# Value sums of three late periods in two halves of the rows, with dense half products between them

## The chip, the core and the metric

The kernel runs on one core of a Trainium2 chip. The metric is the device time of one execution in microseconds, the median of three runs. One more execution was taken with the hardware profiler; its trace is what the times of single instructions come from.

## What is computed

The reference mixes two branches of the same input x (2048 tokens, 512 features) by a gate per token. Branch a is softmax attention with 32 heads of 16 features, branch b a gated layer of width 1792:

```
q, k, v = split(x @ wqkv)                         # 32 heads of 16
p = softmax(q @ k^T / 4);  a = (p @ v) @ wo
b = (sigmoid(x @ w_gate) * (x @ w_up)) @ w_down
g = sigmoid(sum(x * gate_w));  out = g * a + (1 - g) * b
```

All of it is float32. Dense products are made of split operands (a high and a low part, three products for one), in the fast float32 form of TensorE; the value sums p @ v are in plain float32, which TensorE runs in two passes for each product.

## The kernel before

**Periods.** The attention runs in 256 periods (`NPER`), k from 0 to 255, sixteen for each of 16 pairs of heads. Period k takes two key tiles of 128 keys, 1024 queries and the two heads of its pair. Its scores are eight products of 64 rows on 512 queries (line 679, `st_part`): four for the first head of the pair on TensorE's rows 0 to 63 (`t0`, period k) and four for the second on rows 64 to 127 (`t1`, made one period ahead, for k + 1). ScalarE takes the exponential of each into a tile `p` (line 681). `values(k)` (line 823) then sums over the keys: for each of the two key tiles (a = 0, 1) four products of 128 rows, one for each head and half of the queries (c = 3 to 0), with 16 value columns and a column of ones, so 17 columns, which go to partitions 32c of one bank (line 831). The sum leaves its bank by `put` (line 836 on ScalarE, from period 245 on line 838 on VectorE) and is added to a running sum on GpSimd, one period later (line 848).

**Dense half products.** Beside the scores, which use half of TensorE's rows, dense products of the other branches run in halves of the rows. `Sum.half(g)` (line 159) gives one product of 64 rows, on the lower rows (`d0`, g = 0) or the upper (`d1`, g = 1); a `Sum` has six of each, which add up in the one bank `dn`. Where a `Sum` goes from the upper rows to the lower, or back, `turn` (line 171) puts an empty instruction on GpSimd that waits for the last product of the one half, and the first of the other half waits for it: both halves write one bank and must not do so at once. When a `Sum` is done, the next one is fetched from a generator (line 911), and in fetching it the finished one is copied out of `dn` (line 469; from period 245 on that copy, `leave`, is on VectorE). In the last periods the Sums are those of the heads' output projection (`hp`, weights `wo0`, `wo1`).

**Order.** Every engine but the DMA queues runs in the order in which the program issues. The order within a period is written by hand as a string of words, which `emit` (line 870) reads: `t0` and `t1` a score product with its exponential, `d0` and `d1` a half product, `m0` and `m1` a product for the maxima of a later period with its reduction on VectorE, `turn` the change of rows, together with GpSimd's waiting work of about 2 us. `STEADY` serves the periods before 245 (`FREE`) and holds six `d1` and six `d0`, one `Sum` for each period. `LAST` serves the eleven periods from 245 on, in which no maxima are left:

```
LAST = "t0 d1 t0 d1 t0 d1 turn t0 t1 t1 d0 t1 d0 t1 d0"
```

With three `d1` and three `d0` a `Sum` takes two periods: 245 and 246, 247 and 248, and so on to 253 and 254. Behind the words of a period come, in this order: the fetch of the next `Sum` if one is done, or a `turn` if one is half done; GpSimd's waiting work (line 916); `values(k)` (line 925); and from period 245 on three steps of `early` (line 939), VectorE's work on the first hidden tiles (lines 761 to 774: reciprocals, products, splits). In these periods score products and value sums take their banks in turn from the seven banks other than `dn` (`bank7`, line 709).

**After the periods** come the down products (line 1021) with the value sum of period 255 between them, which fill TensorE to the end of the kernel, and the rest of the output projection.

Of the kernel before, what the change touches and what calls it, by code (L numbers as in the profile page):

```python
# [21 lines left out]
SHARED = "both halves of the PE write one bank"  # L22
SYNC = mybir.DependencyInfo(mybir.DependencyClass.Sync, mybir.DependencyReason.DATA)

S, D, H, DH, F = 2048, 512, 32, 16, 1792
P = 128
# [5 lines left out]
VW = DH + 1  # L32
# [6 lines left out]
FREE = NPER - LEAD // 2  # L39
# [7 lines left out]
def gated_mix(ctx, tc, x, xT, wqk, wv, wo, w_gate, w_up, w_down, gate_w, out):  # L47
    nc = tc.nc
    pe, act, dve, pool, sp = nc.tensor, nc.scalar, nc.vector, nc.gpsimd, nc.sync
# [121 lines left out]
    def turn(*runs):  # L171

        token = pool.nop()
        tc.add_manual_dep(token.ins, runs[-1].last.ins.name, SYNC, reason=SHARED)
        for r in runs:
            r.token = token
# [5 lines left out]
    def work(length):  # L182
        length -= over[0]
        while length > 0.3 and (later or turnover or slow):
            cost, step = (later or turnover or slow).pop(0)
            step()
            length -= cost
        over[0] = max(0.0, -length)
# [6 lines left out]
    v = va.rearrange("p (t c) -> p t c", t=NS)  # L195
# [45 lines left out]
    def load_pair(p, cols=slice(0, S)):  # L241
        for t, src in enumerate((q_d, k_d)):
            for b in range(2):
                rows, r = slice((2 * p + b) * DH, (2 * p + b + 1) * DH), 64 * b
                to = (QS, KS)[t][p % 2]
                if t == 0:
                    two, one = src[:, rows, cols].rearrange("a d s -> d a s"), src[0, rows, cols]
                else:
                    two, one = src[0, rows, cols].unsqueeze(1), src[1, rows, cols]
                    two = two.to_broadcast([DH, 2, cols.stop - cols.start])  # L250
                sp.dma_start(to[r:r + 2 * DH, cols].bitcast(F32), two)
                sp.dma_start(to[r + 2 * DH:r + KM, cols].bitcast(F32), one)
# [367 lines left out]
    for c in range(NC):  # L620
# [19 lines left out]
        for i, m in order:  # L640
            o, ops, dst = two[i]
# [26 lines left out]
    def st_part(k, b):  # L668

        p, r = divmod(2 * k, 32)  # L670
        i, kt = divmod(r, 16)
        qs, ks = QS[p % 2], KS[p % 2]
        r = 64 * b
        pt = ptile[k, b] = mid(f"p{k}_{b}")
        for a in range(2):
            for c in range(2):
                o = bank()
                q0 = i * 1024 + c * 512
                pe.matmul(o, ks[r:r + KR, (kt + a) * P:(kt + a + 1) * P], qs[r:r + KR, q0:q0 + 512],  # L679
                          start=True, stop=True)  # L680
                act.activation(pt[:, 2 * a + c, :], o, AF.Exp, scale=DH ** -0.5)  # L681
                yield
# [29 lines left out]
    def hidden_load(c, f):  # L712
        gu = big(f"gul{c}_{f}").rearrange("p (a f s) -> p a f s", a=2, f=2)
        for a in range(2):
            sp.dma_start(gu[:, a], gu_d[a, f:f + 2, :, c * 512:(c + 1) * 512].rearrange("f p s -> p f s"))
        return gu
# [78 lines left out]
    def split_load(r):  # L795
        f, t, c = r // 8, r // 4 % 2, r % 4
        e = split_in[r] = keep.tile([P, 2, 512], F32R, name=f"sq{r}", tag="ev", bufs=2)
        sp.dma_start(e[:, 0, :].bitcast(F32), s_d[t, f, :, c * 512:(c + 1) * 512])

    def split_sum(r):  # L800
        f, t, c = r // 8, r // 4 % 2, r % 4
        e = split_in.pop(r)

        def store():
            for a in range(2):
                sp.dma_start((q_d, k_d)[t][a, (2 + f) * P:(3 + f) * P, c * 512:(c + 1) * 512],
                             e[:, 1 - a, :].bitcast(F32))
        split_later(e[:, 1, :], e[:, 0, :], e[:, 0, :].bitcast(F32), store)
# [3 lines left out]
    def logit_load(t):  # L812
        tok[t] = keep.tile([P, 2, D], F32, name=f"xn{t}", tag="ev", bufs=2)
        sp.dma_start(tok[t], x[t * P:(t + 2) * P, :].rearrange("(t p) d -> p t d", p=P))

    def logits(t, a):
        xn = tok[t][:, a, :]
        dve.tensor_tensor_reduce(xn, xn, gwb, scale=1.0, scalar=0.0, op0=ALU.mult, op1=ALU.add,
                                 accum_out=logit[:, t + a:t + a + 1])
# [3 lines left out]
    def values(k):  # L823

        o = bank()
        half = divmod(k // 8, 2)
        pts = [ptile.pop((k, b)) for b in range(2)]
        for a in range(2):
            for c in reversed(range(4)):
                h = 2 * half[0] + c // 2  # L830
                pe.matmul(o[32 * c:32 * c + VW, :], v[:, 2 * k % 16 + a, h * VW:(h + 1) * VW],  # L831
                          pts[c // 2][:, 2 * a + c % 2, :], start=(a == 0), stop=(a == 1))

        def put(e):
            if 2 * k + LEAD < NSTEP:
                act.activation(e, o, AF.Copy)  # L836
            else:
                dve.tensor_copy(e, o)
        if half not in sums:
            sums[half] = keep.tile([P, 512], F32, name=f"sum{half[0]}_{half[1]}", tag="sum", bufs=2)  # L840
            put(sums[half])
        else:
            e = keep.tile([P, 512], F32, name=f"part{k}", tag="part", bufs=2)
            put(e)
            later.append((1.3, lambda s=sums[half]: add(s, e)))

        def add(s, e):
            pool.tensor_tensor(s, s, e, ALU.add)  # L848
            if k % 8 == 7:
                sp.dma_start(pv_d[half[1], half[0]], s)  # L850

    def mx(b):
        for j in range(LEAD, NSTEP):
            one = sm_step(j)
            for i in range(2):
                one(b, i)
                yield
# [5 lines left out]
    def dense(g):  # L863
        while run:
            run.half(g)
            yield
# [3 lines left out]
    def emit(order, **parts):  # L870

        for word in order.split():
            if word == "turn":
                if run:
                    turn(run)
                work(2.0)
            else:
                kind, _, b = word.partition(":")
                spot[:] = [seven[int(b)]] if b else []
                next(parts[kind], None)  # L880

    STEADY = ("m1:3 t0:2 m0:4 d1 d1 t0:5 m0:6 d1 d1 t0:1 d1 m0:3 d1 t0:2 turn m0:0 t1:4 "
              "m1:5 d0 d0 t1:1 t1:6 d0 m1:2 d0 m1:3 d0 t1:4 d0")
    SUMS = 0
    LAST = "t0 d1 t0 d1 t0 d1 turn t0 t1 t1 d0 t1 d0 t1 d0"

    parts = {"m0": mx(0), "m1": mx(1), "d0": dense(LOW), "d1": dense(UP)}
# [3 lines left out]
    for k in range(NPER):  # L891
        n = 2 * k
        if n + LEAD == NSTEP:
            bank = bank7
            leave = dve.tensor_copy
        if 75 <= k < 123:
            t, r = divmod(k - 75, 6)
            if r in (0, 3):
                split_load(2 * t + r // 3)
            if r in (1, 4):  # L900
                split_sum(2 * t + r // 3)
            if r == 1:
                logit_load(2 * t)
            if r in (3, 4):
                logits(2 * t, r - 3)
        if n % 32 == 0 and n // 32 + 1 < NPAIR:
            load_pair(n // 32 + 1)
        parts["t0"], parts["t1"] = st_part(k, 0), st_part(k + 1, 1) if k + 1 < NPER else iter(())
        emit(STEADY if k < FREE else LAST, **parts)
        if run and run.done():  # L910
            run = next(fill, None)
        elif run and run.n:
            turn(run)
        for half in list(mrow):
            later[:0] = put_max(half)
        work(2.6)
        later.extend(soon)
        soon.clear()
        if k == NPER - 1:
            break  # L920
        if NPER - 16 < k <= NPER - 12:
            for _ in range(2):
                next(next(exps))
        spot[:] = [seven[SUMS]]
        values(k)
        if k == NPER - 17:
            loaded.extend(hidden_load(*chunks[m]) for m in range(2))
            early = [hidden_early(m) for m in range(2)]
            exps = iter([early[0]] * 4 + [early[1]] * 4)
        if 192 <= k < 215 and k % 8 != 4:  # L930
            next(dens[0], None)
        if k == NPER - 6:
            next(dens[1])
        if k == NPER - 2:
            raws = [late_raw(*late[m][:2]) for m in range(2)]
        if k == NPER - 13:
            early = chain(*early)
        if k >= NPER - 13:
            for _ in range(1 if k < FREE else 3):
                next(early, None)  # L940
# [135 lines left out]
```

## Time and profile before

| | |
|---|---|
| median of three runs | 1687.55 us (1686.72 to 1687.7) |
| profiled execution | 1686.04 us |
| its span, first to last instruction | 1684.2 us |
| around the span | 1.8 us |
| granted TensorE clock | 1.000 |
| value sums of 128 rows (line 831), passes in the whole run | 4016 |
| the sums of 246, 248 and 250 start at | 1460.44, 1468.32, 1476.05 us |
| the last value sum (period 255) starts at | 1497.74 us |

How to read the lines that follow: `PE` is TensorE's products, `PEld` its loads of weights, `DVE` VectorE, `ACT` ScalarE, `POOL` GpSimd. A row of the timeline is start and duration in us, engine, line, operation, output<-inputs by the names of the program's tiles, partitions and elements, and how many instructions are merged in the row; `64*128 64x512` is a product with 64 rows, 128 columns and 512 streamed elements. `sm` and `st` are the seven banks, `dn` the eighth. A bracket at the end gives the idle time before, and what ended it. In the table of stretches each engine has its busy time and, in brackets, its instructions, followed by the granted clock, the share of DMA time and GB/s. A product's end is modelled, so the starts are what to compare: consecutive products overlap by their last part.

### The profile page before, as it was taken

To read this page: it belongs to the slowest core of one execution; us is meant where nothing else is said; L and a number is where in the kernel's file an instruction comes from. 1 tells how busy PE (TensorE), PEld (TensorE's weight loads), DVE (VectorE), ACT (ScalarE), POOL (GpSimd) and SP (SyncE) were. 2 spreads that over 40 slices of the span, in tenths; PEclk is the share of its full clock that TensorE was granted. 3 is DMA by queue.
4 is the path that set the end of the run, shared out by engine and by line. 5 is a ranking of instruction groups with operands and counts; after the bars stand their busy time and mean duration, and the time that the engine had idled before them with its cause. 6 is when DMAs were issued, how large, how long until landed. Compare 5 with 4: busy or idle time off the path is not lost.

```text
span 1684.2 us, 34636 instructions
## 1 busy us (share of the span) xinstructions
PE 1678.3 (100%) x12485; PEld 1027.5 (61%) x12485; DVE 1453.4 (86%) x2347; ACT 1362.5 (81%) x2657; POOL 938.9 (56%) x920
## 2 busy tenths in 40 slices
PE   9999999999999999999999999999999999999998
PEld 7755555555555555555555555555555555568887
DVE  7988888888889999999888888889999888888753
ACT  4188898988988898889898989889898989985331
POOL 1134476547666666566666767676666667543010
PEclk9999999999999999999999999999999999999999
DMA  7512446366565564566635353434343435369862
GB/s 240 148 47 59 129 172 211 133 164 209 147 195 139 161 150 156 162 164 186 162 102 146 102 146 108 134 104 132 108 133 106 132 114 165 116 209 287 288 202 69
DMA packets 143755, 254.19 MB, mean 151 GB/s; under 512 B 24224, under 2 KB 36512, under 8 KB 140704
## 3 DMA queue, kind: packets, MB, share of 16 engines
q1 hardware_dynamic: 135968, 237.30, 46.9%
q10 hardware_dynamic: 7616, 14.68, 2.8%
q8 instruction: 98, 1.61, 0.4%
q14 instruction: 73, 0.60, 0.1%
HBM read 149.42 MB, written 102.50 MB: 150 GB/s over the span
## 4 chain that ended last, share of the span: by engine, by line
PE 99%; POOL 0%; issue 0%; ACT 0%; DVE 0%; POOLq 0%
PE dn L162 31%; PE sm L831 27%; PE sm L292 12%; PE st L679 7%; PE sm L1021 5%; PE sm L679 5%; PE st L292 2%; PE dn L1021 2%; PE st L162 2%; PE st L1021 2%; PE st L643 1%; PE st L149 1%; PE sm L149 1%; PE st L831 1%; PE st L85 0%; POOL wd_l L104 0%
## 5 line engine op out<-in xcount | busy, mean ns | idle before, releaser
L294 DVE TENSOR_REDUCE stat<-sm 128x1 f32<-128x512 f32 x1313 | 849.7, 683 | 140.9 <-PE sm L679 124.5
L681 ACT ACTIVATE p<-st 128x512 f32<-128x512 f32 x1019 | 616.1, 650 | 1.1 <-PE st L679 0.6
L681 ACT ACTIVATE p<-sm 128x512 f32<-128x512 f32 x1027 | 609.1, 629 | 0.5 <-PE sm L679 0.2
L292 PE MATMUL sm<-ks,qs 48*128 48x512 f32 x1313 | 515.9, 435 | 0.0
L294 DVE TENSOR_REDUCE stat<-st 128x1 f32<-128x512 f32 x735 | 480.2, 681 | 0.1
L831 PE MATMUL sm<-p,v 128*17 128x512 f32 x4016 | 479.9, 595 | 0.0
L679 PE MATMUL sm<-qs,ks 64*128 64x512 f32 x1027 | 427.7, 419 | 0.0
L679 PE MATMUL st<-qs,ks 64*128 64x512 f32 x1019 | 426.0, 419 | 0.0
L292 PEld LDWEIGHTS sm<-ks,qs 48*128 48x128 f32 x1313 | 234.0, 184 | 290.9 <-DVE stat L294 210.4
L848 POOL TENSOR_TENSOR sum<-sum,part 128x512 f32<-128x512 f32 x224 | 288.8, 1289 | 135.7 <-PE sm L679 120.9
L292 PE MATMUL st<-ks,qs 48*128 48x512 f32 x735 | 290.3, 395 | 0.0
L831 PEld LDWEIGHTS sm<-p,v 128*17 128x17 f32 x4016 | 93.0, 96 | 225.6 <-issue 155.1
L836 ACT ACTIVATE part<-sm 128x512 f32<-128x512 f32 x214 | 128.3, 599 | 125.4 <-issue 84.5
L542 POOL TENSOR_TENSOR chain<-chain,chain 128x512 f32<-128x512 f32 x96 | 124.1, 1293 | 156.0 <-PE sm L679 136.1
L679 PEld LDWEIGHTS st<-qs,ks 64*128 64x128 f32 x1019 | 187.4, 184 | 29.2 <-issue 3.4
L679 PEld LDWEIGHTS sm<-qs,ks 64*128 64x128 f32 x1027 | 189.5, 185 | 9.2 <-issue 5.1
L542 POOL TENSOR_TENSOR had<-chain,had 128x512 f32<-128x512 f32 x96 | 123.6, 1287 | 39.7 <-PE sm L679 17.9
L292 PEld LDWEIGHTS st<-ks,qs 48*128 48x128 f32 x735 | 137.2, 187 | 0.7 <-ACT v L662 0.3
L607 ACT ACTIVATE chain<-dn 128x512 f32<-128x512 f32 x128 | 88.3, 690 | 0.0
L542 POOL TENSOR_TENSOR side<-side,side 128x512 f32<-128x512 f32 x32 | 41.4, 1293 | 77.7 <-PE sm L679 69.1
L104 POOL TENSOR_TENSOR ol<-ot,oh 128x512 fp32r<-128x512 f32 (+1 forms) x8 | 14.2, 1778 | 105.1 <-ACT oh L101 80.5
L319 POOL CAST mhl<-mt 128x32 fp32r<-128x32 f32 x32 | 7.6, 237 | 103.7 <-DVE mt L300 103.7
(913 smaller groups left out, 3225.7 us busy)
## 6 DMA issues: line engine op xcount, KB each, us to landing
gul<-gu_d SPq DMA_DIRECT2D x56, 512.0 KB
had<-gu_d SPq DMA_DIRECT2D x84, 256.0 KB
gu_d<-had SPq DMA_DIRECT2D x84, 256.0 KB
gu_d<-side SPq DMA_DIRECT2D x56, 256.0 KB
pv_d<-sum SPq DMA_DIRECT2D x32, 256.0 KB
qs<-q_d SPq DMA_DIRECT2D x30, 256.0 KB
ks<-k_d SPq DMA_DIRECT2D x30, 256.0 KB
gu_d<-far SPq DMA_DIRECT2D x28, 256.0 KB
```

The costliest lines, as they stand in the source:

```text
L149: pe.matmul(o, a, b, start=(i == 0), stop=(i == len(ops) - 1))
L162: mm = pe.matmul(self.o, a[rows], b[rows], start=(self.n == 0), stop=(self.n == 2 * len(self.ops) - 1))
L292: pe.matmul(t, qs[r:r + KM, qt * P:(qt + 1) * P], ks[r:r + KM, g * 512:(g + 1) * 512], start=True, stop=True)
L294: dve.tensor_reduce(stat[half][:, b, qt % 8, g:g + 1], t, axis=AX.X, op=ALU.max)
L542: pool.tensor_tensor(to, u, w, ALU.add)
L607: leave = lambda e, o: act.activation(e, o, AF.Copy)
L679: pe.matmul(o, ks[r:r + KR, (kt + a) * P:(kt + a + 1) * P], qs[r:r + KR, q0:q0 + 512], start=True, stop=True)
L681: act.activation(pt[:, 2 * a + c, :], o, AF.Exp, scale=DH ** -0.5)
L831: pe.matmul(o[32 * c:32 * c + VW, :], v[:, 2 * k % 16 + a, h * VW:(h + 1) * VW], pts[c // 2][:, 2 * a + c % 2, :], start=(a == 0), stop=(a ...
L836: act.activation(e, o, AF.Copy)
L848: pool.tensor_tensor(s, s, e, ALU.add)
L1021: pe.matmul(down[t], a, b, start=(f == 0 and m == 0), stop=(f == NF - 2 and m == 5))
```

## The change

In periods 246, 248 and 250 (`APART`) `values(k)` is made in two halves of the rows. The lower half (rows 0 to 63, the first 64 keys of each tile) takes eight products of 64 rows, four for a = 0 and four for a = 1; behind the first four stand two `d1`, the upper half products of the `Sum` just fetched, and behind the second four a third one. Then an empty instruction on GpSimd waits for the last product of the lower half; the first product of the upper half (rows 64 to 127) waits for it, and eight more products complete the sum. In the period after each of these (247, 249, 251), `NEXT` takes the place of `LAST`: the same words without the three `d1`. The other periods are unchanged, as are the exponentials, the copies out of the banks and every step of VectorE and GpSimd but the three empty instructions.

```diff
         pts = [ptile.pop((k, b)) for b in range(2)]
-        for a in range(2):
+        def part(rows, a, start, stop):
             for c in reversed(range(4)):
                 h = 2 * half[0] + c // 2
-                pe.matmul(o[32 * c:32 * c + VW, :], v[:, 2 * k % 16 + a, h * VW:(h + 1) * VW],
-                          pts[c // 2][:, 2 * a + c % 2, :], start=(a == 0), stop=(a == 1))
+                mm = pe.matmul(o[32 * c:32 * c + VW, :], v[rows, 2 * k % 16 + a, h * VW:(h + 1) * VW],
+                               pts[c // 2][rows, 2 * a + c % 2, :], start=start, stop=stop)
+                if token:
+                    tc.add_manual_dep(mm.ins, token.pop().ins.name, SYNC, reason=SHARED)
+            return mm
+
+        token = []
+        if k in APART:
+            for a in range(2):
+                mm = part(slice(0, 64), a, a == 0, False)
+                for _ in range(2 - a):
+                    next(parts["d1"])
+            token.append(pool.nop())
+            tc.add_manual_dep(token[0].ins, mm.ins.name, SYNC, reason=SHARED)
+            for a in range(2):
+                part(slice(64, P), a, False, a == 1)
+        else:
+            for a in range(2):
+                part(slice(0, P), a, a == 0, a == 1)
...
     SUMS = 0
+    APART = (246, 248, 250)
+    NEXT = "t0 t0 t0 turn t0 t1 t1 d0 t1 d0 t1 d0"
     LAST = "t0 d1 t0 d1 t0 d1 turn t0 t1 t1 d0 t1 d0 t1 d0"
...
-        emit(STEADY if k < FREE else LAST, **parts)
+        emit(STEADY if k < FREE else NEXT if k - 1 in APART else LAST, **parts)
```

## The prediction

> **What bounds the kernel now.** I read the engine totals first, then busy time by stretches, then the order of time around the three changed periods.
>
> ```profile
> PE 1678.3 (100%) x12485; PEld 1027.5 (61%) x12485; DVE 1453.4 (86%) x2347; ACT 1362.5 (81%) x2657; POOL 938.9 (56%) x920
> ```
>
> ```profile
> core 0: us, PE busy (x) PEld busy (x) DVE busy (x) ACT busy (x) POOL busy (x), PEclk, DMA share, GB/s
> 1456.60:1491.80 35.20, 35.20 (x272) 16.70 (x271) 27.85 (x39) 35.20 (x73) 13.33 (x12) 1.00 0.24 78
> ...
> 1500.00:1520.00 20.00, 19.92 (x87) 15.91 (x86) 17.93 (x12) 11.12 (x14) 13.89 (x7) 1.00 1.01 348
> 1520.00:1540.00 20.00, 20.00 (x89) 16.52 (x88) 16.61 (x14) 8.68 (x9) 8.19 (x3) 1.00 0.95 302
> 1580.00:1600.00 20.00, 20.00 (x90) 16.57 (x89) 15.55 (x17) 6.55 (x7) 1.30 (x1) 1.00 0.84 262
> ```
>
> TensorE is busy all the time, and the down products after 1500 us run at 90 in 20 us with no gap to fill; 87 and 89 in the two stretches before leave room for 3 + 1 products, some 0.9 us. So time lost before 1500 us reaches the end, less 0.9 us at most. The last periods, the first row, are where the change sits. There ScalarE is as full as TensorE: 73 exponentials in 35.2 us.
>
> ```profile
> 1456.60 1.91 PE L831 MATMUL sm<-p,v 128*17 128x512 f32 x16
> ...
> 1491.80 1.92 PE L831 MATMUL st<-p,v 128*17 128x512 f32 x16
> ```
>
> ```profile
> 1476.10 0.85 ACT L681 ACTIVATE p<-sm 128x512 f32<-128x512 f32 x1
> 1476.57 0.86 ACT L681 ACTIVATE p<-st 128x512 f32<-128x512 f32 x1
> 1477.05 0.87 ACT L681 ACTIVATE p<-sm 128x512 f32<-128x512 f32 x1
> 1477.53 0.89 ACT L681 ACTIVATE p<-st 128x512 f32<-128x512 f32 x1
> 1478.01 0.90 ACT L681 ACTIVATE p<-sm 128x512 f32<-128x512 f32 x1
> 1478.57 0.83 ACT L681 ACTIVATE p<-st 128x512 f32<-128x512 f32 x1
> ```
>
> The first two rows are the value sums of periods 245 and 254: nine periods in 35.2 us, 3.91 us each. The exponentials start 0.475 us apart, so eight of them take 3.80 us: ScalarE leaves 0.1 us of a period. The sum of period 250 starts at 1476.05; five exponentials follow it, and the sixth (1478.57), the first on a score product made after the sum, comes 0.08 us late. So ScalarE's backlog covers the present length of a value sum and not more.
>
> Now the price of a value sum and of its neighbours.
>
> ```profile
> 1479.83 0.39 PE L162 MATMUL dn<-wo0h,xl 64*128 64x512 f32 x1
> 1480.15 1.91 PE L831 MATMUL sm<-p,v 128*17 128x512 f32 x16
> ...
> 1481.99 0.49 PE L679 MATMUL st<-qs,ks 64*128 64x512 f32 x1
> ...
> 1482.33 0.39 PE L679 MATMUL sm<-qs,ks 64*128 64x512 f32 x1
> ...
> 1482.56 0.39 PE L679 MATMUL st<-qs,ks 64*128 64x512 f32 x1
> ```
>
> ```profile
> 1481.45 0.61 PE L831 MATMUL sm<-p,v 128*17 128x512 f32 x4
> ```
>
> Sixteen passes go in four rounds of four; the last round starts 1.30 us after the first, so a round is 0.433 us. From the last round to the next score product are 0.54 us, 0.11 more than a round; from the last dense half product to the sum 0.32 us, 0.09 more than the 0.23 of the steps between half products; and the first half product behind a sum takes 0.34, not 0.23 (its weights weren't loaded ahead). So a change from the narrow form (17 columns) to the wide (128 columns) and back costs 0.1 us on each side and 0.11 on the first wide product. From S, the start of a sum, to the next score product are 1.84 us.
>
> **The change part by part.** (1) *Two halves.* Each sum becomes 16 products of 64 rows for 8 of 128. Their passes stream the same 512 columns; no row shows 64 rows with 17 columns, and I take the 0.433 us round of the 128-row form (a 64-row score product, 0.23, streams as fast as a 128-row down product: 20.00 us over 88 steps). Between the ends "half a round" and "sixteen in a row" it is the nearest row.
>
> (2) *A dense half product ahead of its time.* The three upper half products of a new sum leave the next period's head for the middle of the value sum. The new sum goes into the one bank dn, which VectorE must first empty (L469). Before, that copy had the whole value sum to finish in.
>
> ```profile
> 1460.44 1.91 PE L831 MATMUL sm<-p,v 128*17 128x512 f32 x16
> ...
> 1461.77 0.63 DVE L469 COPY hp<-dn 128x512 f32<-128x512 f32 x1
> ...
> 1462.51 0.18 PEld L162 LDWEIGHTS dn<-wo0h,xh 64*128 64x128 f32 x1
> ```
>
> ```profile
> 1468.32 1.91 PE L831 MATMUL st<-p,v 128*17 128x512 f32 x16
> ...
> 1469.37 0.68 DVE L469 COPY hp<-dn 128x512 f32<-128x512 f32 x1
> ...
> 1470.16 0.18 PEld L162 LDWEIGHTS dn<-wo0h,xh 64*128 64x128 f32 x1
> ```
>
> ```profile
> 1474.26 0.69 DVE L838 COPY part<-st 128x512 f32<-128x512 f32 x1 [1.56 <-PE st L831]
> ...
> 1475.33 1.82 DVE L774 TENSOR_TENSOR xl<-gul,xh 128x512 fp32r<-128x512 f32 x1
> ...
> 1476.05 1.99 PE L831 MATMUL sm<-p,v 128*17 128x512 f32 x16
> ...
> 1477.06 0.41 DVE L761 TENSOR_SCALAR gul<-gul 128x512 f32<-128x512 f32 x1
> ...
> 1477.40 0.68 DVE L469 COPY hp<-dn 128x512 f32<-128x512 f32 x1
> ...
> 1478.19 0.18 PEld L162 LDWEIGHTS dn<-wo0h,xh 64*128 64x128 f32 x1
> 1478.22 0.47 PE L162 MATMUL dn<-wo0h,xh 64*128 64x512 f32 x1
> 1478.22 0.18 PEld L679 LDWEIGHTS sm<-qs,ks 64*128 64x128 f32 x1
> ```
>
> The copy starts late because VectorE, in order, has the last sum's eviction (L838) and three steps of the early hidden tiles ahead of it, and the diff moves none of these. dn is free for the first half product 0.11 us after the copy: G = 1462.51, 1470.16 and 1478.19, that is S + 2.07, S + 1.84 and S + 2.14, **6.05 us** together, where the four low products ahead of it have issued by S + 0.43. A waiting half product holds what is behind it: the last two rows show a score product's weights let in only 0.03 us behind those of the half product that waited. So behind it wait the other low products, the upper half, the next scores, and through these ScalarE's exponentials.
>
> (3) *From G on*, if the narrow and the wide form exclude each other also at 64 rows: second half product at +0.34; low products for a = 1 at +0.66 (0.32); their second round +0.43, third half product +0.54, at G + 1.63; upper half after a single first product, 0.34 - 0.23 + 0.32 = 0.43, at G + 2.06; next score product 1.84 later, at **G + 3.90**. Before it stood at S + 1.84. The loss is G - S + 2.06 in each of three sums: 6.05 + 6.18 = **12.2 us**.
>
> (4) *The token.* An existing one costs:
>
> ```profile
> 1482.56 0.39 PE L162 MATMUL dn<-wo1h,xl 64*128 64x512 f32 x1
> ...
> 1483.09 0.49 PE L162 MATMUL dn<-wo1h,xh 64*128 64x512 f32 x1
> ```
>
> The upper half product ends at 1482.95, the lower one starts 0.14 us later. The new token lies beside the third half product (0.43), so I count nothing. POOL is in order, and at 246 stands there with
>
> ```profile
> 1462.96 1.30 POOL L136 TENSOR_TENSOR xl<-of,xh 128x512 fp32r<-128x512 f32 x1
> ```
>
> which ends at 1464.26; the upper half is due at 1462.51 + 2.06 = 1464.57, so it is still covered, by 0.3 us. Behind the nop on POOL are the next turn and the partial sums (L848); they have a period to spare.
>
> (5) *NEXT* keeps its eight scores and three lower half products, so its seven rounds stay; what goes is the wait of its first half product. Periods 247 and 251 took 4.03 us (1460.44 to 1464.47) and 4.10 (1476.05 to 1480.15), 249 took 3.83 (1468.32 to 1472.15).
>
> ```profile
> 1464.47 1.91 PE L831 MATMUL st<-p,v 128*17 128x512 f32 x16
> ...
> 1472.15 1.97 PE L831 MATMUL st<-p,v 128*17 128x512 f32 x16
> ```
>
> ScalarE's 3.80 is the floor, so the relief is at most 0.23 + 0.30 + 0.03 = **0.6 us**, which I take.
>
> The sum is 12.2 - 0.6 = **+11.7 us** (11.67 unrounded): 1686.04 of the profiled execution becomes 1697.7. The runs' median, 1687.55, is 1.5 us above it; against that median **1699.2 us**.
>
> The Trainium skill, TensorEngine Tiling (Array Packing), section "Tiling Modes", lists 64x32 and 64x128 as separate modes and says that "changing tiling mode (not just tile) drains the TensorE". The 0.1 us on each side of a sum agree with it for 128x32; no run shows it for 64x32 yet. By it the sum is that of (3), and without it that of the first rival.
>
> **The rivals.** *Side by side:* the 64-row products run beside dense half products on the other rows, as scores and dense half products do. The wait for dn stays, 6.05 us. From G: second half product +0.34, low products at once with it, last round at +0.77, done 0.61 later at G + 1.38, token 0.14, upper half at G + 1.52, next score beside its last round (+1.30) at G + 2.82. Loss 6.05 + 3 x (2.82 - 1.84) = 9.0, less 0.6: +8.4, **1696.0**. For it: scores and dense half products of 64 rows each start together. Against it: narrow and wide forms have 0.1 us between them here wherever they meet. Were dn also free in time, the low half would end at S + 1.91, the upper start at S + 2.05, the score at S + 3.35: 4.5 - 0.6 = +4.0, 1691.5.
> The Trainium skill, TensorE: Matmul & The Clock Gate, Part 3, tells of tiles in different row and column groups running at once, with 10.6x for sixteen of them; that speaks for this rival, and no row here has such a mix.
>
> *One strip after the other:* sixteen passes of a half in a row, 6.9 us for 1.7: 5.2 x 6 more, 1730. Against it: the 128-row form runs four at once.
>
> *Not slower:* ScalarE paces these periods. If the exponentials pending at S outlasted the split sum, TensorE's longer way would cost nothing: 1687.5. It decides when the pending work exceeds today's by the 3.9 us per sum, eight exponentials beside the five, thirteen in all. Against it: the scores take turns in seven banks, one of which is the value sum's, so six can be pending; and the late sixth exponential above.
>
> **How the numbers follow.** Forecast 0.58, side by side 0.30 (with dn in time or not), one after the other 0.04, longer changes of form 0.04, not slower 0.04. The low end is side by side with dn free in time, 1691.5. The high end prices the twelve added changes of form (six for two, three times) at 0.3 us above today's 0.1: +3.6, 1703. A difference under 0.2%, 3.4 us, can hardly be told from none: faster 0.01, same 0.03, slower 0.96.
>
> **What would show it.** In the profile after: L162's first upper half product in the middle of the sums of 246, 248 and 250, 1.8 to 2.1 us after S and 0.1 behind L469, with TensorE idle before it; the sum's 64-row products not overlapping L162 products, about 5.7 to 6.0 us from S to the next score; ScalarE idle some 4 us three times; the other periods as before, and the down stage's shape unchanged, only later. Wrong would be: low products under way during L162's (side by side), an L469 moved ahead of the early steps, narrow products no longer four at once, or down products that win back more than 0.9 us.

## The result, and the profile after

The changed kernel takes **1709.5 us** (median of four runs, 1706.3 to 1711.13) against 1687.44 us before: the ratio is 1.0128, 95% interval 1.0117 to 1.014, so 22 us slower. The forecast was 1699.2 us with a range up to 1703: the direction was right, the loss nearly twice as large as forecast (22.1 us for 11.7). The profiled execution took 1706.3 us, its span 1704.4. Three executions that ran far slower than all others (1758.75 and 3164.95 us of the kernel before, 3170.29 us of the experiment with period 246 alone) are left out of every time below.

First one stretch of both kernels, from the start of the value sum of 246 to that of 252, by busy time; the column behind the brackets is the granted clock. Before:

```profile
1460.44:1483.98 23.54, 23.54 (x181) 11.09 (x180) 19.18 (x28) 23.54 (x49) 9.52 (x9) 1.00 0.29 93
```

After:

```profile
1461.52:1504.12 42.60, 39.68 (x230) 14.77 (x229) 19.14 (x28) 24.22 (x49) 9.56 (x9) 0.80 0.16 52
```

The stretch is 19.06 us longer. All but 1.2 of the 20.3 us between the two profiled executions lies in it; 1.08 us stood already ahead of it (the sum of 246 starts at 1461.52, not 1460.44), where nothing was changed. TensorE stands still for 2.9 us, and the clock, 1.00 before, has a mean of 0.80. Cut where the clock changes:

```profile
1474.04:1477.46 3.42, 2.68 (x19) 0.74 (x19) 0.87 (x2) 2.00 (x5) 0.00 (x0) 1.00 0.49 171
1477.46:1484.28 6.82, 6.82 (x31) 2.82 (x27) 2.32 (x4) 3.19 (x7) 0.00 (x0) 0.50 0.01 3
1484.28:1487.70 3.42, 3.42 (x33) 1.61 (x26) 1.72 (x3) 2.25 (x5) 0.76 (x1) 1.00 0.00 0
1487.70:1491.11 3.41, 2.29 (x19) 0.54 (x18) 2.02 (x3) 2.62 (x6) 0.53 (x1) 1.00 0.35 74
1491.11:1501.35 10.24, 10.24 (x44) 3.51 (x44) 2.70 (x4) 4.03 (x8) 1.32 (x1) 0.50 0.31 105
...
1600.00:1620.00 20.00, 20.00 (x90) 16.57 (x89) 15.55 (x17) 6.55 (x7) 1.30 (x1) 1.00 0.85 273
```

The clock is halved twice, for 6.82 and 10.24 us. TensorE is busy all through both, but with slower products. The down products are as before, 90 in 20 us. Now the sums themselves, on TensorE; a bracket is a wait. The sum of 246, at full clock:

```profile
1461.52 1.05 PE L831 MATMUL sm<-p,v 64*17 64x512 f32 x8
1463.62 0.46 PE L162 MATMUL dn<-wo0h,xh 64*128 64x512 f32 x1 [1.06 <-DVE hp L469]
1463.93 0.39 PE L162 MATMUL dn<-wo0l,xh 64*128 64x512 f32 x1
1464.25 1.05 PE L831 MATMUL sm<-p,v 64*17 64x512 f32 x8
1465.23 0.50 PE L162 MATMUL dn<-wo0h,xl 64*128 64x512 f32 x1
1465.66 1.91 PE L831 MATMUL sm<-p,v 64*17 64x512 f32 x16
1467.50 0.51 PE L679 MATMUL sm<-qs,ks 64*128 64x512 f32 x2
```

The sum of 248:

```profile
1473.18 1.05 PE L831 MATMUL st<-p,v 64*17 64x512 f32 x8
1474.96 0.49 PE L162 MATMUL dn<-wo0h,xh 64*128 64x512 f32 x1 [0.74 <-DVE hp L469]
...
1477.03 3.25 PE L831 MATMUL st<-p,v 64*17 64x512 f32 x16
1480.21 0.79 PE L679 MATMUL sm<-qs,ks 64*128 64x512 f32 x1
```

And that of 250:

```profile
1487.68 1.05 PE L831 MATMUL sm<-p,v 64*17 64x512 f32 x8
1489.86 0.46 PE L162 MATMUL dn<-wo0h,xh 64*128 64x512 f32 x1 [1.12 <-DVE hp L469]
...
1492.47 3.61 PE L831 MATMUL sm<-p,v 64*17 64x512 f32 x16
1496.01 0.81 PE L679 MATMUL st<-qs,ks 64*128 64x512 f32 x2
```

From the start of a sum to the next score:

| sum | forecast (G - S + 3.90) | measured | row of the upper half (x16), 1.91 at full clock |
|---|---|---|---|
| 246 | 5.97 | 5.98 | 1.91 |
| 248 | 5.74 | 7.03 | 3.25 |
| 250 | 6.04 | 8.33 | 3.61 |

In 246 every step is as forecast, G at S + 2.10 and G + 3.88 to the next score. In the others the wait is as forecast too (S + 1.78, S + 2.18); what is longer is what runs at half clock. ScalarE runs dry meanwhile: its first exponential behind the sum of 246 comes after 3.78 us without work, some 4 us as forecast; behind the sums of 248 and 250, with the clock halved, it waits 5.05 and 6.58 us.

```profile
1468.10 0.60 ACT L681 ACTIVATE p<-sm 128x512 f32<-128x512 f32 x1 [3.78 <-PE sm L679]
```

### The profile page after: what moved, and what is told of

The parts are those of the page before. It is cut to its first block, busy times and chain, and to the rows that moved or that the text cites. A ratio compares the mean times of both kernels' runs of the same rounds, so it can differ in the third digit from the quotient of the medians.

```text
span 1704.4 us, 34735 instructions
## 1 busy us (share of the span) xinstructions
PE 1695.3 (99%) x12533; PEld 1032.5 (61%) x12533; DVE 1451.5 (85%) x2347; ACT 1363.0 (80%) x2657; POOL 936.6 (55%) x920
## 5 line engine op out<-in xcount | busy, mean ns | idle before, releaser
L831 PE MATMUL sm<-p,v 128*17 128x512 f32 (+1 forms) x4048 | 487.0, 598 | 0.0
L831 PEld LDWEIGHTS sm<-p,v 128*17 128x17 f32 (+1 forms) x4048 | 93.8, 97 | 229.1 <-issue 158.0
L679 PEld LDWEIGHTS sm<-qs,ks 64*128 64x128 f32 x1027 | 189.8, 186 | 10.4 <-issue 5.9
```

The lines of the kernel that those rows point to most:

```text
L831: mm = pe.matmul(o[32 * c:32 * c + VW, :], v[rows, 2 * k % 16 + a, h * VW:(h + 1) * VW], pts[c // 2][rows, 2 * a + c % 2, :], start=start, ...
```

## Experiments

The question was what halves the clock. Theories: **idle**, the 0.7 to 1.1 us of standing still for dn; **half rows**, the narrow products of 64 rows, little work for the array; **both**, that it takes the two in one stretch. Each run is compared with the kernel before on the same chip (1687.26 us for the first four, 1687.07 for the others).

**The split alone.**

```diff
         if k in APART:
             for a in range(2):
                 mm = part(slice(0, 64), a, a == 0, False)
-                for _ in range(2 - a):
-                    next(parts["d1"])
...
-        emit(STEADY if k < FREE else NEXT if k - 1 in APART else LAST, **parts)
+        emit(STEADY if k < FREE else LAST, **parts)
```

> The value sums of 246, 248 and 250 in two halves with the token between them, but no dense half products inside and LAST in every late period. Of the steps only the second half is left: last round 1.30 + 0.61 + token 0.14 = 2.05 us more for each sum, +6.2 us in all. TensorE waits for nothing longer than the token (0.3 us). If the 1 us of standing still in mid-sum is what brings the granted clock down (theory idle), the clock stays at 1.00 and the time is 1693.5. If it is the half-row products themselves, little work for the array over 3.9 us in a row (theory half rows), the clock falls to 0.5 after at least one of the three and the time is 1698 to 1702. If it takes both in one stretch, 1693.5.

1693.19 us, ratio 1.0035 (1.0023 to 1.0048), clock 1.00. In the stretch from 246 to 252 it loses 6.1 us, as worked out. In 246 the token comes late, behind GpSimd's other work, and TensorE waits 0.64 us for it, not 0.3 at most, as the second L831 row shows:

```profile
1460.54 1.92 PE L831 MATMUL sm<-p,v 64*17 64x512 f32 x16
1463.10 1.91 PE L831 MATMUL sm<-p,v 64*17 64x512 f32 x16 [0.64 <-POOLq L841]
```

Half rows alone for 3.9 us in a row don't halve the clock.

**Dense products between, whole rows.**

```diff
             for a in range(2):
-                mm = part(slice(0, 64), a, a == 0, False)
+                part(slice(0, P), a, a == 0, a == 1)
                 for _ in range(2 - a):
                     next(parts["d1"])
-            token.append(pool.nop())
-            tc.add_manual_dep(token[0].ins, mm.ins.name, SYNC, reason=SHARED)
-            for a in range(2):
-                part(slice(64, P), a, False, a == 1)
```

> The three upper dense half products stay in the middle of the sums of 246, 248 and 250 and NEXT stays, but the sums keep their 128 rows and need no token. TensorE stands 0.8 to 1.1 us for dn as in the changed kernel. Steps: G - S 6.05, then G + 1.97 to the next score against S + 1.84, 0.4 more, less 0.6: +5.8 us. Theory idle: the clock falls to 0.5 after one or more of the waits, 1698 to 1702. Theory half rows, and also the theory that it takes both: clock 1.00, 1693.2.

1691.75 us, ratio 1.0026 (1.0015 to 1.0037), clock 1.00 in all seven executions. TensorE's wait is that of the changed kernel to 0.01 us in 246:

```profile
1461.23 1.05 PE L831 MATMUL sm<-p,v 128*17 128x512 f32 x8
1463.34 0.46 PE L162 MATMUL dn<-wo0h,xh 64*128 64x512 f32 x1 [1.05 <-DVE hp L469]
```

So the wait alone, at this length, doesn't halve it either. The stretch from 246 to 252 is 28.05 us, 4.5 more than before, 1.3 less than worked out: in 246 the third half product and the next score start together (both at 1464.95), where the steps put one behind the other, which is 0.36 us less in that sum.

**The copy ahead.**

```diff
-            for _ in range(1 if k < FREE else 3):
+            for _ in range(1 if k < FREE else 0 if k + 1 in APART else 6 if k in APART else 3):
                 next(early, None)
```

> The changed kernel with VectorE's three early steps of 245, 247 and 249 moved behind the next sum's copy (six in 246, 248 and 250), so that dn is free about 1 us after the start of the sum and TensorE stands still for 0.2 us at most. Half products, order and token as in the changed kernel. Steps: start of sum to next score 4.9 us against 1.84, +9.1 - 0.6 = +8.5 us. Theory idle, and also the theory that it takes both: clock 1.00, 1696. Theory half rows: clock 0.5 after at least one, 1700 to 1705.

1703.88 us, ratio 1.0089 (1.0071 to 1.0108), clock 0.996 in the profiled execution (1704.04 us). One of the four executions kept its clock, with a mean of 1.000, and took 1697.45 us; the other three, at 0.995 and 0.996, took 1703.72 to 1704.68. The same kernel is 6 to 7 us faster where the clock isn't halved. At first sight the halving speaks for half rows. But the run didn't do what it was made for: the six steps hold up VectorE's put of 247 (here line 855), that holds a bank, and TensorE stands still elsewhere.

```profile
1467.50 5.00 DVE L765 RECIPROCAL gul<-gul 128x128 f32<-128x128 f32 x6
1472.42 0.63 DVE L855 COPY part<-st 128x512 f32<-128x512 f32 x1
```

```profile
1471.45 0.49 PE L162 MATMUL dn<-wo1h,xh 64*128 64x512 f32 x1
1473.10 0.50 PE L679 MATMUL st<-qs,ks 64*128 64x512 f32 x1 [1.16 <-DVE part L855]
```

The clock halves right behind this wait, at 1474.69, with only the first 0.9 us of the split sum of 248 run, and comes back 13.65 us later:

```profile
1471.27:1474.69 3.42, 2.26 (x18) 0.72 (x14) 2.47 (x4) 3.42 (x9) 1.28 (x1) 1.00 0.00 0
1474.69:1488.34 13.65, 13.65 (x58) 4.18 (x54) 4.53 (x7) 4.54 (x10) 0.00 (x0) 0.50 0.12 44
```

It decides nothing between the theories, except against "half rows" as the only cause: the two split sums without a wait, 246 and 250, kept the clock at 1.00.

**The lower half in one piece.**

```diff
             for a in range(2):
                 mm = part(slice(0, 64), a, a == 0, False)
-                for _ in range(2 - a):
-                    next(parts["d1"])
+            for _ in range(3):
+                next(parts["d1"])
             token.append(pool.nop())
```

> The changed kernel with the lower half in one piece: eight low products, then the three upper dense half products, token, upper half. The wait for dn lies behind the low products (1.84 us) and is 0.3 us or less; two changes of form go. Steps: from G 0.89 to the upper half, 1.84 more, so G - S + 0.89 a sum: 6.05 + 2.7 - 0.6 = +8.1 us. Theory idle, and the theory that it takes both: clock 1.00, 1695.5. Theory half rows: clock 0.5 after at least one, 1700 to 1705.

1694.62 us, ratio 1.0044 (1.0029 to 1.0059), clock 1.00. The same products and the same token as in the changed kernel, in another order, 15 us faster: the wait is 0.2 us. This is what idle and both forecast (1695.5), and it speaks against half rows.

```profile
1460.98 1.92 PE L831 MATMUL sm<-p,v 64*17 64x512 f32 x16
1463.08 0.46 PE L162 MATMUL dn<-wo0h,xh 64*128 64x512 f32 x1 [0.19 <-DVE hp L469]
```

**The wait filled.**

```diff
         if k in APART:
+            part(slice(0, P), 0, True, True)
             for a in range(2):
                 mm = part(slice(0, 64), a, a == 0, False)
```

> The changed kernel with four more products of 128 rows ahead of each split sum: the a = 0 products once more, whole, overwritten by the low ones that follow. They add two rounds, 0.87 us, just where TensorE stood still for dn, so the dense half product meets a free dn and the wait falls to 0.3 us or less. All later half products stay as in the changed kernel. Theory both (the clock falls where standing still and half-row products meet in one stretch of 3.4 us): clock 1.00 and about 1698.7 us, the +11.4 of the steps alone, so the kernel with more work is some 11 us faster than the changed one. Theory half rows: the clock still falls, 1704 to 1712. Theory idle: clock 1.00.

1698.69 us, ratio 1.0072 (1.0058 to 1.0086): **10.8 us less than the changed kernel, with twelve products more** (10.4 us less when each is set against the kernel before in its own runs). The split sums and what stands between their halves are unchanged; only the wait has work in it. The forecast of half rows alone, 1704 to 1712, is out.

```profile
1461.31 2.03 PE L831 MATMUL sm<-p,v 128*17 128x512 f32 x16
1463.42 0.46 PE L162 MATMUL dn<-wo0h,xh 64*128 64x512 f32 x1
```

The first row merges the four added products and the first four low ones. The stretch from 246 to 252, full clock throughout:

```profile
1461.31:1496.24 34.93, 34.72 (x253) 12.60 (x253) 19.20 (x28) 23.77 (x49) 9.60 (x9) 1.00 0.20 63
```

34.93 - 23.54 = 11.4 us: this is the price of the steps without the clock, which the forecast put at 11.7. One of the four executions had a mean clock of 0.997 and took 1701.36; it wasn't traced.

**Whole rows and a longer wait.**

```diff
+        if k >= FREE:
+            leave = (lambda e, o: act.activation(e, o, AF.Copy)) if k in APART else dve.tensor_copy
         if run and run.done():
             run = next(fill, None)
```

(on the run with whole rows)

> The run with whole rows and dense half products between them, but the copy out of dn in 246, 248 and 250 on ScalarE behind its pending exponentials instead of on VectorE: dn free about 3.2 us after the start of the sum, not 2.0, so TensorE stands still for some 2.2 us three times, without a half-row product. Steps: +1.2 us a sum more than that run, 1695.3. If the clock goes by the share of the array's rows at work over 3.4 us, whichever way it is lost (theory both, as a share): 0.3 or less in some stretches, clock 0.5 after at least one, 1699 to 1706. If half-row products are needed for it: clock 1.00, 1695.3.

1699.21 us, ratio 1.0074 (1.0059 to 1.0088). The waits are 2.1 to 2.4 us, and the clock halves behind the first of them, without any 64-row value product:

```profile
1461.68 1.05 PE L831 MATMUL sm<-p,v 128*17 128x512 f32 x8
1465.11 0.47 PE L162 MATMUL dn<-wo0h,xh 64*128 64x512 f32 x1 [2.38 <-ACT hp L926]
```

```profile
1463.05:1466.46 3.41, 1.35 (x10) 0.43 (x10) 0.05 (x1) 1.92 (x4) 2.27 (x3) 1.00 0.19 72
1466.46:1469.88 3.42, 3.42 (x16) 2.22 (x12) 2.74 (x4) 2.03 (x5) 1.28 (x1) 0.50 0.02 6
```

So half rows aren't needed: a long wait does it as well. "Both" holds only in the form of a share of work that can be lost in either way.

**Period 246 alone.**

```diff
-    APART = (246, 248, 250)
+    APART = (246,)
```

> The change in period 246 alone. Steps: the sum longer by G - S 2.07 + 2.06 = 4.1 us, the next period 0.35 shorter: +3.8 us, 1691.1, at clock 1.00. Theory both: where the stretch of 3.4 us happens to hold the wait and the half-row products together, some runs have the clock at 0.5 for 7 to 10 us and are 3 to 4 us longer, 1694 to 1695.

1694.85 us, ratio 1.0049 (1.003 to 1.0068): some 8 us for one sum, where its steps at full clock were put at 3.8. In the profiled execution (1694.73) the clock halves for 6.83 us in the middle of the sum, at 1466.13:

```profile
1462.72:1466.13 3.41, 2.61 (x19) 0.85 (x23) 0.66 (x2) 1.49 (x4) 2.34 (x3) 1.00 0.22 79
1466.13:1472.96 6.83, 6.83 (x35) 2.77 (x27) 3.17 (x4) 3.49 (x8) 1.28 (x1) 0.50 0.00 0
```

The same sum kept its clock in the profiled execution of the changed kernel: the stretches in which the work is weighed don't start with the program's steps.

**The kernel before, with its copy earlier.**

```diff
-            for _ in range(1 if k < FREE else 3):
+            for _ in range(1 if k < FREE else 2 if k % 2 else 4):
```

> The kernel before with VectorE's early steps from 245 on two in odd periods and four in even ones, for three and three, so that the copy out of dn comes some 0.9 us earlier and the dense half products at the head of 247, 251 and 253 don't wait. Their periods were 4.03, 4.10 and 3.97 us where the others take 3.83 to 3.90. If these waits lie on the path: -0.3 to -0.6 us, 1686.9. If VectorE's put comes late in the even periods instead: 0 to +0.5 us.

1687.43 us against 1687.07, ratio 1.0002 (0.9992 to 1.0011): no difference that can be told. The copies do come earlier (in 246 at 0.52 us behind the start of the sum, not 1.33), but the periods take 3.91 us on average in both kernels. The late half products at the head of 247 and 251 cost the kernel before nothing as a whole. No version beats the kernel before.

**What the clock goes by.** All halvings begin on one grid of 3.41 us in each execution, which gives the stretches to compare. From the products' starts I worked out for each stretch of eight profiled executions (1440 to 1512 us) which share of the array's rows was at work: a wide product counts 0.227 us, a narrow round of four 0.433 us, each by its rows of 128. In the stretch 1487.70 to 1491.11 of the changed kernel that is 0.85 us of low rounds, two half products of 0.227 and 0.63 us of low rounds, all on half the rows: (0.85 + 0.45 + 0.63) / 2 / 3.41 = 0.28.

| stretch at clock 1.00 | share of rows | share of time with any product | the clock next |
|---|---|---|---|
| whole rows, long wait, 1463.05 | 0.27 | 0.34 | 0.50 |
| changed kernel, 1487.70 | 0.28 | 0.58 | 0.50 |
| changed kernel, 1474.04 | 0.29 | 0.60 | 0.50 |
| 246 alone, 1462.72 | 0.31 | 0.63 | 0.50 |
| copy ahead, 1471.27 | 0.36 | 0.52 | 0.50 |
| whole rows, long wait, 1473.29 | 0.37 | 0.42 | 1.00 |
| wait filled, 1463.12 | 0.39 | 0.80 | 1.00 |
| changed kernel, 1460.39 | 0.40 | 0.62 | 1.00 |
| all others | 0.42 and more | | 1.00 |

The share of rows parts the five stretches that were followed by half clock from all others; the share of time doesn't (0.42 kept it, 0.63 lost it). The highest share that lost the clock, 0.36, and the lowest that kept it, 0.37, are close together, and the count gives every product a fixed length: the bound lies near there, and isn't better known than that. It was read off these stretches afterwards; what was on record before a run, that of the long wait, is only its form, a share of rows that a wait lowers as well, with 0.3 or less as the sign.

The whole of all ten traces bears it out. Counted again from 10 us on (the figures come out up to 0.01 above the table's), 13 stretches at full clock were followed by half clock and held 0.367 or less, and 4898 were followed by full clock and held 0.380 or more. One stretch of each kind, near the kernel's end, holds 128-row down products alone and no half rows: 0.367 in the split alone, followed by half clock, and 0.394 in the copy ahead, followed by full clock.

```profile
1684.68:1688.09 3.41, 1.41 (x7) 0.83 (x5) 1.50 (x2) 0.00 (x0) 0.00 (x0) 1.00 0.51 193
1688.09:1690.29 2.20, 0.00 (x0) 0.00 (x0) 0.00 (x0) 0.00 (x0) 0.00 (x0) 0.50 0.16 59
```

```profile
1696.56:1699.97 3.41, 1.50 (x7) 0.92 (x5) 1.50 (x2) 0.00 (x0) 0.00 (x0) 1.00 0.48 183
1699.97:1702.25 2.28, 0.00 (x0) 0.00 (x0) 0.00 (x0) 0.00 (x0) 0.00 (x0) 1.00 0.19 71
```

The end of a half clock goes with the same count. Products take nearly twice as long there (dense half products start 0.425 us apart, for 0.23), and each still counts its full-clock time. Seven stretches at half clock held 0.20 to 0.38 and were followed by another; five held 0.39 to 0.47 and were followed by full clock. By these figures, as an estimate, products on half the rows alone come to 0.27 at most at half clock (0.227 of 0.425 us, on half the rows), too little to end it. No run was made to try this.

## Why the prediction missed

1. **What bounds the kernel**: right. The down products stayed at 90 in 20 us, and 20.1 us of loss at the start of the sum of 252 were 20.3 at the end: nothing was won back.
2. **Half products stream like whole ones**: right. At full clock a narrow round of 64 rows takes what one of 128 takes (x16 in 1.91 us). The table of the kernel before has 4016 passes of these sums; those are the ones into banks named `sm`, and 80 more go into `st`.
3. **The wait for dn**: right, 2.10, 1.78 and 2.18 us behind the start of the sum for 2.07, 1.84 and 2.14, and the low products for a = 1 did wait behind it.
4. **Narrow and wide forms exclude each other**: right. From the last half product to the next narrow one are 0.32 us and back 0.55, and in 246 no L162 product starts before the narrow round ahead of it has had its 0.433 us; side by side is ruled out. The rule of the Trainium skill, TensorEngine Tiling (Array Packing), section "Tiling Modes", that a change of mode drains TensorE, agrees with these steps for 64x32 beside 64x128.
5. **The token and NEXT**: right in size. The steps together cost 11.4 us at full clock (the wait filled) for 11.7. The relief in NEXT was a little larger than ScalarE's pace was thought to allow: period 247 has 1.83 us from its first score to its sum, against 2.18 before, 0.35 less for the 0.23 that was counted.
6. **The step that failed** is a term that the sum put at nothing without a reason, the clock: every duration was taken from rows at clock 1.00, and the clock was assumed to stay there, with the range's high end left to the changes of form alone. In the profiled execution half clock costs 19.06 - 11.4 = 7.7 us: 1.3 and 2.3 in the sums of 248 and 250 (the table above), the rest in 249 and 251, whose own sums took 2.28 and 2.90 us for 1.91. The 6 to 7 us between executions of the copy ahead, with 13.65 us of half clock in its trace for 17.06 here, fit that. The median, at 22 us, has some 3 us more; the other three executions weren't traced, but their mean clocks, 0.991 to 0.993 for 0.994, point the same way. The prediction itself had the 1 us of standing still and the half-empty array, side by side in one sum; what it lacked was that the two together, 0.28 and 0.29 of the rows over a stretch of 3.41 us, halve the clock for the next ones.

My first theories were also too narrow: neither idle nor half rows nor the need for both stood up to the long wait with whole rows.

## What to carry to other kernels

Before a step lowers TensorE's work for a few microseconds, by waits or by products that fill part of the rows, add up the share of the rows at work over some 3.4 us: here 0.37 or less was followed by 3 to 14 us at half clock, and for period 246 alone that cost as much as the step itself. Work that another engine must release belongs behind work that is free, as the lower half in one piece showed: the same products in another order gave 15 us back. Halving the rows of a product halves none of its time; it can pay only where the other half has work at the same time, as the scores and dense half products have here, both 128 columns wide.

## What was not expected of the hardware

- The clock halved after stretches of 3.41 us in which TensorE had a product under way for as much as 0.63 of the time (by the profile's modelled ends 0.78, 2.68 of 3.42 us from 1474.04), and behind a wait as short as 0.74 us, in the sum of 248. The Trainium skill, TensorE: Matmul & The Clock Gate, Part 1, puts the window at about 3.4 us and free-running, with which the grid here agrees; its rule to have no idle gaps over some 3.4 us is too mild for these rows.
- Half clock lasted one, two, three or four such stretches (3.4, 6.8, 10.2, 13.7 us), though TensorE was busy all through them: its end, too, went with the share of rows at work, 0.39 and more.
- A kernel with twelve products more was 10.8 us faster than the same kernel without them.
